# Reordering an attention and gated-convolution kernel with a list scheduler, whole-batch operations and full-array matmuls

## The chip, the cores and the metric

The kernel runs on one core of a Trainium2 chip. The metric is the device time of the whole program in microseconds (us), median of several executions, after its result was compared with the reference. For one core, an execution counts as slow when it is over 1.5% above the fastest of the same kernel. Engine names in profile lines: PE is TensorE (matmul), PEld its weight loads, DVE is VectorE, ACT is ScalarE, POOL is GpSimd (here it mostly issues loads), SP is SyncE. PSUM is the memory that the matmuls write to; these kernels use it in a few buffers, which ACT or DVE reads out before the next matmul may write there. The granted clock is the share of its full speed that the chip allowed TensorE. A matmul uses a part of TensorE's array of 128 rows and 128 columns; the size of that part is called its tile size.

## The reference

Eight batches, eight heads, 576 tokens, head size 64. Keys and values are averaged over groups of 8 tokens (72 remain), attention follows, and its output (512 columns a token) feeds a network with a three-tap convolution along the tokens as its gate.

```python
k_p = k.reshape(B, H, 72, 8, D).mean(axis=3)          # v_p likewise
attn = softmax(q @ k_p.T / sqrt(D))
x = (attn @ v_p)                                      # -> B, 576, 512
h = np.maximum(x @ w_in, 0)                           # 512 -> 1024 ("first layer")
gate = sigmoid(sum(conv_w[k] * shifted(h, k) for k in range(3)))
out = (h * gate) @ w_out                              # 1024 -> 512 ("second layer")
```

## The kernel before

Heads are handled in pairs. The order is written by hand: attention steps of batch b+1 stand between feed-forward steps of batch b. The parts that matter here, with cuts marked `# ...`:

```python
q_sb = qsb_pool.tile([96, S // 96, 2, D], BF16, name="q_sb")
for hh in range(2):
    nc.gpsimd.dma_start(out=q_sb[:, :, hh, :],
        in_=q[b, h0 + hh, :, :].rearrange("(c p) d -> p c d", p=96))   # runs of 256 bytes
# ... scores: each head of the pair uses 64 rows of the array
scps = sc_psum.tile([Sp, SC], FP32, name="scps", tag="sc")             # 2 buffers, SC = 288
nc.tensor.matmul(out=scps, lhsT=kT_sb[pb:pb + D, :], rhs=qT_sb[pb:pb + D, c0:c0 + SC], ...)
nc.scalar.activation(out=attnTs[hh][:, c0:c0 + SC], in_=scps, func=ACT.Exp, scale=...)
# ... attention times v; token tiles of 128,128,128,128,64
nc.vector.reciprocal(out=r_sb[0:usz], in_=avt[0:usz, sl, :, D])
for hh in range(2):
    nc.vector.tensor_scalar(out=x_pair[...], in0=avt[...], scalar1=r_sb[0:usz, hh:hh + 1], op0=OP.mult, ...)
# ... feed-forward: per block of 128 columns and per 288 tokens
#   first layer: 4 matmuls, relu on ACT;  convolution: 3 matmuls with diagonal weights, tanh on ACT
#   (the convolution's PSUM tiles share the two "sc" buffers with the scores)
for b in range(B):                     # the hand-written order, cut
    ffn_mm1(b, 2); ffn_conv(b, 1)
    attn_scores(nxt, 0)
    ffn_mm1(b, 3); ffn_conv(b, 2)
    attn_av(nxt, 0); attn_prep(nxt, 1); attn_loads(nxt, 3)
    # ...
```

The softmax here doesn't subtract the row's maximum and nothing guards it: scores larger than these inputs give would overflow.

## Time and profile before

Three executions: 328.02 to 329.11 us, median 328.87. From the page of the profiled execution (span; busy time and share of each engine; busy tenths of TensorE in 40 slices; the chain of work that ended last by engine and by line; groups of instructions with busy time, mean ns of one, and idle time in front of them; the issues of the q load):

```profile
span 327.8 us, 6104 instructions
PE 289.7 (88%) x2080; PEld 166.7 (51%) x2080; DVE 213.5 (65%) x904; ACT 188.3 (57%) x473; POOL 103.0 (31%) x196
...
PE   0054669999999999999999999999999999999995
...
PE 79%; DMA 11%; ACT 3%; DVE 3%; POOL 2%; issue 1%; ACTq 0%; POOLq 0%
PE hps L273 22%; PE cps L293 15%; PE scps L191 8%; DMA q_sb<-in_q_dram 5%; PE avps L223 5%; PE xt_ps L252 3%; PE q_ps L173 2%; DMA convw<-in_moe_conv_w_dram 2%; ACT xT L255 2%; DMA k_raw<-in_k_dram 2%; DMA w_in_sb_119<-in_moe_w_in_dram 1%; DVE osb L336 1%; DMA out_dram<-osb 1%; PE kT_ps L162 1%; DVE x_pair L234 1%
...
L234 DVE TENSOR_SCALAR x_pair<-avps,r_sb 128x64 bf16<-128x64 f32 (+1 forms) x320 | 72.3, 275 | 0.5
...
L198 ACT ACTIVATE attnT<-scps 72x288 bf16<-72x288 f32 x128 | 51.0, 405 | 12.8 <-PE scps L191 9.5
...
q_sb<-in_q_dram POOLq DMA_DIRECT2D x64, 72.0 KB, 3.8
```

Read it so. PE has 88% of the span and most of the chain: TensorE bounds the kernel. The slices show where it does not: about 50 us at the start. DVE spends its largest share on 320 normalizations of 64 columns, ACT runs exponentials in calls of 288 columns, and q comes in 64 small issues.

A busy share does not tell whether TensorE does useful work, because records of pipelined matmuls overlap and also cover waits inside the array. So I took the distance from one matmul's start to the next from the trace. Its usual value where nothing interferes is the floor of a kind of matmul. The sums include every wait in front of the next matmul.

```
kind                                    floor      before, us in all   after, us in all
first layer, convolution (288 columns)  122-125 ns      131.0              112.3
second layer (512 columns)              216 ns           74.4               63.8
scores (288 columns)                    122 ns           37.3               19.3
attention times v (65 columns)           33 ns           20.1               15.9
transposes of 128 columns                56 ns           (all three kinds of transposes: 53.2 before, 34.5 after)
```

In steady batches of the kernel before, a batch takes 35.8 us; its floors sum to about 28. The lines below are TensorE in one such stretch (timeline: start in us, duration, engine, line of the kernel, operation, output and inputs, rows*columns of the array used, count):

```profile
164.07 0.28 PE L273 MATMUL hps<-xT,w_in_sb_116 128*128 128x288 bf16 x1
164.37 0.28 PE L191 MATMUL scps<-qT_sb,kT_sb 64*72 64x288 bf16 x1
164.58 0.30 PE L273 MATMUL hps<-xT,w_in_sb_117 128*128 128x288 bf16 x1
164.71 0.29 PE L273 MATMUL hps<-xT,w_in_sb_118 128*128 128x288 bf16 x1
164.93 0.31 PE L191 MATMUL scps<-qT_sb,kT_sb 64*72 64x288 bf16 x1
165.17 0.30 PE L273 MATMUL hps<-xT,w_in_sb_119 128*128 128x288 bf16 x1
```

First-layer matmuls (128 rows) alternate with scores (64 rows). From 164.58 to 164.71, between two first-layer matmuls, the step is 0.13 us. The steps into and out of a scores matmul take 0.21 to 0.30.

### The profile page before, as it was taken

Reading aid. Unit: us, or ns where it says so; the run is one execution under the profiler, and the core shown is the slowest. Engines: PE = TensorE matmul, PEld = TensorE weight load, DVE = VectorE, ACT = ScalarE, POOL = GpSimd, SP = SyncE. Lnnn points to the kernel's source line nnn. Section 1 sums busy time; section 2 is a strip of 40 time slices with the busy share of each in tenths; the row PEclk is TensorE's granted clock in tenths of the full one; section 3 lists DMA queues with packets and bytes.
Section 4 is the critical chain, followed back from the end, with each engine's and each line's share of the span. In section 5 each row is a group of like instructions: output and inputs, shape, how many; then the busy total and the mean of one; then the engine's idle time right before and its main releaser. Section 6 shows DMA issues by size and latency. Waiting matters only on the chain.

```text
span 327.8 us, 6104 instructions
## 1 busy us (share of the span) xinstructions
PE 289.7 (88%) x2080; PEld 166.7 (51%) x2080; DVE 213.5 (65%) x904; ACT 188.3 (57%) x473; POOL 103.0 (31%) x196
## 2 busy tenths in 40 slices
PE   0054669999999999999999999999999999999995
PEld 0032335664566446654656456554566455645752
DVE  3523883677857785778757785777667866675452
ACT  1068425883398509872587429860787348852940
POOL 8068997752442226042513233110000000000000
PEclk9999999999999999999999999999999999999999
DMA  8999999995693659155964567133100120003003
GB/s 166 173 120 190 150 151 129 147 104 98 125 100 22 84 123 109 31 54 97 135 79 36 82 138 56 8 27 108 40 2 1 66 81 2 0 34 112 2 32 113
DMA packets 57342, 27.28 MB, mean 83 GB/s; under 512 B 42464, under 2 KB 51552, under 8 KB 57312
## 3 DMA queue, kind: packets, MB, share of 16 engines
q0 software_dynamic: 51968, 17.20, 48.2%
q10 hardware_dynamic: 2928, 5.38, 4.9%
q1 hardware_dynamic: 2416, 4.33, 4.5%
q8 instruction: 16, 0.26, 0.3%
q14 instruction: 14, 0.11, 0.1%
HBM read 32.52 MB, written 9.44 MB: 128 GB/s over the span
## 4 chain that ended last, share of the span: by engine, by line
PE 79%; DMA 11%; ACT 3%; DVE 3%; POOL 2%; issue 1%; ACTq 0%; POOLq 0%
PE hps L273 22%; PE cps L293 15%; PE scps L191 8%; DMA q_sb<-in_q_dram 5%; PE avps L223 5%; PE xt_ps L252 3%; PE q_ps L173 2%; DMA convw<-in_moe_conv_w_dram 2%; ACT xT L255 2%; DMA k_raw<-in_k_dram 2%; DMA w_in_sb_119<-in_moe_w_in_dram 1%; DVE osb L336 1%; DMA out_dram<-osb 1%; PE kT_ps L162 1%; DVE x_pair L234 1%
## 5 line engine op out<-in xcount | busy, mean ns | idle before, releaser
L234 DVE TENSOR_SCALAR x_pair<-avps,r_sb 128x64 bf16<-128x64 f32 (+1 forms) x320 | 72.3, 275 | 0.5
L293 PE MATMUL cps<-hT,dw 128*128 128x288 bf16 x384 | 60.3, 288 | 0.0
L255 ACT COPY xT<-xt_ps 128x576 bf16<-128x576 bf16 x32 | 20.4, 637 | 69.0 <-PE xt_ps L252 56.9
L121 POOL DMA_DIRECT2D q_sb<-in_q_dram x64 | 47.9, 759 | 35.7 <-PE q_ps L173 22.5
L231 DVE RECIPROCAL r_sb<-avps 128x2 f32<-128x2 f32 (+1 forms) x160 | 22.9, 161 | 54.4 <-PE avps L223 53.7
L198 ACT ACTIVATE attnT<-scps 72x288 bf16<-72x288 f32 x128 | 51.0, 405 | 12.8 <-PE scps L191 9.5
L280 ACT ACTIVATE hT<-hps 128x288 bf16<-128x288 f32 x128 | 52.0, 413 | 8.1 <-PE hps L273 3.7
L300 ACT ACTIVATE tg<-cps 128x288 bf16<-128x288 f32 x128 | 48.7, 412 | 7.4 <-PE cps L293 7.1
L191 PE MATMUL scps<-qT_sb,kT_sb 64*72 64x288 bf16 x128 | 39.1, 318 | 5.4 <-ACT attnT L198 4.8
L223 PE MATMUL avps<-v_aug,attnT 72*128 72x65 bf16 (+1 forms) x320 | 37.9, 202 | 5.3 <-DVE x_pair L234 4.2
L328 PEld LDWEIGHTS <-gT 128*128 128x128 bf16 (+1 forms) x320 | 27.8, 99 | 26.0 <-DVE gT L321 1.8
L293 PEld LDWEIGHTS <-dw 128*128 128x128 bf16 x384 | 35.3, 98 | 9.7 <-issue 0.2
L223 PEld LDWEIGHTS <-attnT 72*128 72x128 bf16 (+1 forms) x320 | 26.4, 102 | 26.0 <-issue 9.7
L273 PE MATMUL hps<-xT,w_in_sb_116 128*128 128x288 bf16 x128 | 37.5, 295 | 2.3 <-DVE osb L336 1.4
L273 PE MATMUL hps<-xT,w_in_sb_119 128*128 128x288 bf16 x128 | 36.4, 293 | 3.1 <-ACT xT L255 3.1
L273 PE MATMUL hps<-xT,w_in_sb_118 128*128 128x288 bf16 x128 | 37.5, 295 | 0.4 <-ACT xT L255 0.4
L273 PE MATMUL hps<-xT,w_in_sb_117 128*128 128x288 bf16 x128 | 37.4, 294 | 0.4 <-ACT xT L255 0.4
L178 ACT COPY qT_sb<-q_ps 128x576 bf16<-128x576 bf16 x32 | 20.5, 640 | 25.3 <-PE q_ps L173 25.1
L147 POOL MEMSET v_aug<- 72x2 bf16 x32 | 3.3, 110 | 100.2 <-PE avps L223 99.8
L191 PEld LDWEIGHTS <-kT_sb 64*72 64x72 bf16 x128 | 13.4, 109 | 29.2 <-issue 23.1
L252 PE MATMUL xt_ps<-ident_b,x_pair 128*128 128x128 bf16 (+1 forms) x160 | 26.5, 224 | 0.1
L113 POOL DMA_DIRECT2D v_raw<-in_v_dram x28 | 19.8, 707 | 11.5 <-DVE vt_3488 L149 2.6
(719 smaller groups left out, 429.3 us busy)
## 6 DMA issues: line engine op xcount, KB each, us to landing
q_sb<-in_q_dram POOLq DMA_DIRECT2D x64, 72.0 KB, 3.8
out_dram<-osb ACTq DMA_DIRECT2D x16, 256.0 KB
k_raw<-in_k_dram POOLq DMA_DIRECT2D x28, 144.0 KB, 4.5
v_raw<-in_v_dram POOLq DMA_DIRECT2D x28, 144.0 KB, 4.3
out_dram<-osb SPq DMA_DIRECT2D x8, 256.0 KB
out_dram<-osb POOLq DMA_DIRECT2D x8, 256.0 KB, 2.4
v_raw<-in_v_dram ACTq DMA_DIRECT2D x4, 288.0 KB
k_raw<-in_k_dram SPq DMA_DIRECT2D x4, 288.0 KB
```

The source lines that it names most:

```text
L121: nc.gpsimd.dma_start(out=q_sb[:, :, hh, :], in_=q[b, h0 + hh, :, :].rearrange("(c p) d -> p c d", p=96),)
L191: nc.tensor.matmul(out=scps, lhsT=kT_sb[pb:pb + D, :], rhs=qT_sb[pb:pb + D, c0:c0 + SC], start=True, stop=True,)
L198: nc.scalar.activation(out=attnTs[hh][:, c0:c0 + SC], in_=scps, func=ACT.Exp, scale=1.0 / (POOL * 8.0))
L223: nc.tensor.matmul(out=avt[0:usz, sl, hh, :], lhsT=attnTs[hh][:, u0:u0 + usz], rhs=v_aug[:, hh, :], start=True, stop=True,)
L234: nc.vector.tensor_scalar(out=x_pair[0:usz, hh * D:(hh + 1) * D], in0=avt[0:usz, sl, hh, 0:D], scalar1=r_sb[0:usz, hh:hh + 1], scalar2=Non ...
L252: nc.tensor.transpose(out=xt_ps[:, u0:u0 + usz], in_=x_pairs[i][0:usz], identity=ident_b[0:usz, 0:usz])
L255: nc.scalar.copy(out=xT, in_=xt_ps)
L273: nc.tensor.matmul(out=hps, lhsT=w_in_sb[dc][:, fb * P:(fb + 1) * P], rhs=xT_tiles[(b, dc)][:, c0:c0 + SC], start=(dc == 0), stop=(dc == n ...
L280: nc.scalar.activation(out=hT[:, fb, 1 + c0:1 + c0 + SC], in_=hps, func=ACT.Relu, scale=0.5)
L293: nc.tensor.matmul(out=cps, lhsT=dw[:, kk, i, :], rhs=hT[:, fb, c0 + kk:c0 + kk + SC], start=(kk == 0), stop=(kk == 2),)
L300: nc.scalar.activation(out=tg[:, c0:c0 + SC], in_=cps, func=ACT.Tanh, scale=0.5)
L328: nc.tensor.matmul(out=ops_[0:osz, :], lhsT=gT[:, fc, os0:os0 + osz], rhs=w_out_sb[fc], start=(fc == 0), stop=(fc == n_fb - 1),)
```

## The change

Intent: let a scheduler that runs at build time order all operations by engine, with estimated durations and a model of load arrival; make the operations larger (all heads of a batch or of a token tile at once, 576 columns a call on ACT); use only full-array matmuls, so that the array's tile size never changes; load each batch in three large loads with long runs. The core of a diff of 964 lines:

```diff
+class Planner:
+    N_PS = 4;  DMA_RATE = 220e3;  DMA_LAT = 2.2;  SEM = 0.12
+    def order(self):      # repeatedly: among operations whose inputs are planned, per engine the
+        # ...             # earliest start (0.02 us of slack), ties by priority; 4 PSUM buffers of 2 banks
-    nc.gpsimd.dma_start(out=q_sb[:, :, hh, :], in_=q[b, h0 + hh].rearrange("(c p) d -> p c d", p=96))
+    nc.gpsimd.dma_start(out=q_b[m], in_=flat_tokens(q, b))          # 9 KB in a row
-    lhsT=kT_sb[pb:pb + D, :],  rhs=qT_sb[pb:pb + D, c0:c0 + SC]      # 64 rows
+    lhsT=kTz[m][:, par, h*Sp:(h+1)*Sp],  rhs=qT[m][:, :, h*A:(h+1)*A]   # 128 rows, half of kTz is zero
-    for hh in range(2): nc.vector.tensor_scalar(out=x_pair[...], ...)
+    nc.vector.tensor_tensor(out=xx[i3] (128 x 512), in0=av_view(), in1=rr broadcast, op=OP.mult)
-    last token tile: 64 tokens (tokens 512 to 575)
+    last token tile: 128 tokens (448 to 575), overlapping the one before
-    relu / tanh / exp on 288 columns
+    relu / tanh / exp on 2 x 288 columns in one call
-    second layer: 5 token tiles a batch
+    second layer: 9 full token tiles for a pair of batches
+    # ... every operation: pl.add(name, engine(s), duration, fn, reads, writes, prio, ...)
+    with tc.manual_schedule():
+        for s, e, d, o in pl.order():
+            o.fn(e)
```

## The prediction

> **What bounds the kernel now.** TensorE. The page gives PE 289.7 us busy (88%), DVE 65%, ACT 57%, POOL 31%; PE has 79% of the chain that ended last. The timeline shows three stages: a prologue of 50 us, in which PE starts at 16 us, waits for q loads and small vector work, and runs first-layer matmuls at half pace (240 ns each, later 123); seven batches of 35.8 us; a last feed-forward of 24 us.
>
> Busy time hides the real limit, so I took start-to-start distances of matmuls from the trace. Undisturbed: 123 ns for 288 columns (first layer, convolution), 216 for 512 (second layer), 34 for attention times v, 56 for 128-column transposes. In the batch at 121.8 to 157.6 us these floors sum to 28.3 us. The other 7.5: 58 places where the array's tile size changes (64-row scores, 64-row or 64-column last token tiles, 64-column k transposes) lose 6.1 us over the floors, the other 200 lose 1.8. A first-layer matmul followed by a scores matmul takes 225 ns instead of 123, the way back 242. The Trainium skill, "TensorEngine Tiling (Array Packing)", Key Properties, says that a change of tiling mode drains TensorE; this trace agrees, about 0.1 us for each change.
>
> **What the change does.**
> - TensorE: scores contract over 128 zero-padded rows, the last token tile overlaps the one before, the output is tiled over batch pairs (36 tiles, not 40). Nearly all tile-size changes go. Count times floor: 512 and 384 at 123 = 63 + 47; 288 at 216 = 62; 128 scores at 123 = 16; 320 at 34 = 11; 160 and 144 transposes at 56 = 9 + 8; 48 at 42 = 2. Sum 218 us, 27.3 a batch (was 28.3 + 7.5).
> - ACT: 128x288 calls (405 to 413 ns) pair into 128x576 (estimate 0.65 us from the 0.64 us copy of that width): 192 x 0.65 = 125 us.
> - DVE: 320 normalizations at 275 ns become 40 of 128x512, estimate 0.69 each from the equal-sized output copy (28 us instead of 72); reciprocals 23 to 7 us; pooling sums 4.4 us a batch.
> - Copies that go to either add some 80 us. ACT and DVE end near 160 us each, under TensorE.
> - DMA: 256-byte q rows (64 issues) become 9 KB runs; POOL issues fall from 120 to 36; the software queue's 48% share should halve. In the steady state this is off the critical path; in the prologue it counts.
>
> **Prologue.** k, q, v and a quarter of the input weights are 4.1 MB; at the 171 GB/s of the first 16 us, or better with long rows, q and k land near 13 us; attention of batch 0 is paced by eight exponentials (5 us) and five normalization rounds (5 us). I expect the first feed-forward matmul near 28 us, saturated soon after (before: 50).
>
> **Sum.** 28 + (218 - 6 used before) + 1.5 of stall a batch (12) + 2 of half-rate start - 3 of overlap + 4 tail = 255 us. Range 244 to 270. Of the 74 us saved, about 20 come from the prologue, 43 from tile-size changes and other gaps, 8 from fewer columns.
>
> **Right if** the batch period is 28 to 30 us; scores matmuls follow each other and first-layer matmuls at about 123 ns; the chain is over 80% PE; ACT and DVE stay below 70%.
>
> **Wrong if** the strided q operand streams slower than 123 ns; the four two-bank PSUM buffers (estimate: 70% occupied) make PE wait because the fixed order assumes wrong durations; the loads of batch 0 land later; or merged ACT/DVE instructions cost more than estimated.
>
> Chances: faster 0.97, within 2% 0.02, slower 0.01.

## The result, and the profile after

After: 262.14 us median of four executions (260.94 to 262.55), before in the same rounds 328.44. The ratio is 0.796 (95% interval 0.793 to 0.800). Ratios in this document are the mean time of one kernel's fast runs over that of the other's in the same rounds, so not quite the ratio of the medians quoted. The page after, the same parts, and the granted clock by slice in tenths:

```profile
span 259.9 us, 4786 instructions
PE 235.1 (90%) x1985; PEld 166.9 (64%) x1985; DVE 126.8 (49%) x307; ACT 166.5 (64%) x271; POOL 25.6 (10%) x47
...
PE   0488997969999999999999999999999999999992
...
PEclk9995999968999999999999999999999999999999
...
PE 76%; ACT 13%; DVE 6%; DMA 3%; issue 1%; ACTq 0%; POOLq 0%
PE psf L478 24%; PE psf L531 23%; PE psf L497 18%; PE psf L402 5%; ACT tg L504 3%; DMA q_b<-in_q_dram 3%; ACT attnT L413 3%; DVE xx L443 2%; PE psb L385 2%; ACT osb L539 2%; PE psb L457 2%; PE psf L430 1%; ACT xT L463 1%; ACT qT L391 1%; ACT kTz L357 1%
...
L413 ACT ACTIVATE attnT<-psf 72x576 bf16<-72x576 f32 x64 | 39.7, 644 | 1.9 <-PE psf L402 1.9
...
L443 DVE TENSOR_TENSOR xx<-psf,rr 128x512 bf16<-128x512 f32 x40 | 26.8, 684 | 0.4
...
q_b<-in_q_dram POOLq DMA_DIRECT2D x7, 576.0 KB, 6.4
```

The first visible thing is the start: TensorE is saturated from the fifth slice (a slice is 6.5 us here), before from the seventh (of 8.2 us). Merged instructions cost less than the parts that they replace: an exponential of 576 columns 644 ns where two of 288 took 405 each, a normalization of 512 columns 684 ns where eight of 64 took 275 each. The second thing are dents in the seventh and ninth slice, between 39 and 58 us; in the ninth the clock shows a 6 (the 5 in the fourth slice belongs to the start). Nothing in the prediction speaks of them. Where a trace has no clock record, the page shows full clock. There is none before 16.4 us here, and none before 55.5 us in the kernel before, and until 16.2 and 55.1 us matmuls of 288 columns start 240 ns apart, half the later pace; so read no full clock from the first slices. The windows view of the changed kernel (stretch in us, its length, then busy time with count of PE, PEld, DVE, ACT, POOL, mean granted clock, DMA share, GB/s) shows it in figures:

```profile
core 0: us, PE busy (x) PEld busy (x) DVE busy (x) ACT busy (x) POOL busy (x), PEclk, DMA share, GB/s
0.00:23.30 23.30, 11.34 (x101) 8.60 (x102) 14.01 (x41) 12.45 (x23) 14.91 (x32) 0.93 1.14 197
23.30:38.80 15.50, 15.48 (x112) 11.58 (x112) 4.56 (x12) 9.67 (x15) 0.00 (x0) 0.89 1.19 206
38.80:62.10 23.30, 18.89 (x163) 12.74 (x161) 14.36 (x30) 12.66 (x21) 3.45 (x5) 0.85 0.91 159
62.10:90.00 27.90, 27.41 (x267) 21.81 (x265) 19.03 (x43) 23.81 (x41) 3.71 (x5) 1.00 0.67 107
90.00:120.00 30.00, 29.39 (x258) 20.81 (x256) 18.16 (x41) 21.45 (x36) 2.96 (x4) 1.00 0.78 141
```

From 23.3 to 38.8 us the feed-forward of batch 0 runs alone; from 38.8 to 62.1 the attention of batch 1, with only a few second-layer tiles beside it; only then do the two overlap as meant. PE is busy 18.9 of these 23.3 us, at a mean clock of 0.85.

The steady state looks as predicted. The same kind of stretch after the change (TensorE alone in the timeline):

```profile
121.29 1.14 PE L478 MATMUL psf<-xT,w_in 128*128 128x288 bf16 x8
122.27 0.41 PE L402 MATMUL psf<-qT,kTz 128*72 128x288 bf16 x2
122.51 0.91 PE L497 MATMUL psf<-hT,dw 128*128 128x288 bf16 x6
```

Eight first-layer matmuls take 0.98 us (121.29 to 122.27), two scores 0.24, and they follow each other without a gap.

Where the time went, worked out from start-to-start distances in both traces (time over the floors, us; floors for the same 2,080 and 1,985 matmuls; floors are rounded, so each column adds up to 0.3 us over its span):

```
                          before (span 327.8)    after (span 259.9)
sum of floors             223.5                  217.5
start to first steady
  feed-forward            43.1  (0 to 50.3)       17.6  (0 to 23.3)
all after that            57.5                    20.1, of which 9.0 from 38.8 to 62.1
after the last matmul      4.0                     5.0
```

So of the 67.9 us, 25.5 come from the start, 37.4 from the stretch after it, 6.0 from fewer matmul columns; 1.0 is lost at the end.

### The profile page after: what moved, and what is told of

Read it like the earlier page. It is cut to its first block, busy times and chain, and to the rows that moved or that the text cites. A ratio compares the mean times of both kernels' runs of the same rounds, so it can differ in the third digit from the quotient of the medians.

```text
span 259.9 us, 4786 instructions
## 1 busy us (share of the span) xinstructions
PE 235.1 (90%) x1985; PEld 166.9 (64%) x1985; DVE 126.8 (49%) x307; ACT 166.5 (64%) x271; POOL 25.6 (10%) x47
## 3 DMA queue, kind: packets, MB, share of 16 engines
q0 software_dynamic: 15024, 15.67, 38.5%
## 4 chain that ended last, share of the span: by engine, by line
PE 76%; ACT 13%; DVE 6%; DMA 3%; issue 1%; ACTq 0%; POOLq 0%
PE psf L478 24%; PE psf L531 23%; PE psf L497 18%; PE psf L402 5%; ACT tg L504 3%; DMA q_b<-in_q_dram 3%; ACT attnT L413 3%; DVE xx L443 2%; PE psb L385 2%; ACT osb L539 2%; PE psb L457 2%; PE psf L430 1%; ACT xT L463 1%; ACT qT L391 1%; ACT kTz L357 1%
## 5 line engine op out<-in xcount | busy, mean ns | idle before, releaser
L478 PE MATMUL psf<-xT,w_in 128*128 128x288 bf16 x512 | 74.4, 290 | 1.2 <-ACT xT L463 0.5
L531 PE MATMUL psf<-w_out,gT 128*128 128x512 bf16 x288 | 65.9, 379 | 1.4 <-DVE gT L514 1.1
L509 DVE TENSOR_SCALAR tg<-tg 128x576 bf16<-128x576 bf16 x64 | 20.1, 314 | 82.9 <-ACT tg L504 82.3
L478 PEld LDWEIGHTS <-w_in 128*128 128x128 bf16 x512 | 50.3, 99 | 15.7 <-issue 1.5
L497 PE MATMUL psf<-hT,dw 128*128 128x288 bf16 x384 | 57.9, 286 | 1.1 <-ACT kTz L357 1.0
L484 ACT ACTIVATE hT<-psf 128x576 bf16<-128x576 f32 x64 | 41.7, 652 | 18.0 <-PE psf L478 17.6
L531 PEld LDWEIGHTS <-gT 128*128 128x128 bf16 x288 | 27.9, 98 | 32.0 <-DVE gT L514 2.2
L504 ACT ACTIVATE tg<-psf 128x576 bf16<-128x576 f32 x64 | 41.5, 649 | 7.7 <-PE psf L497 2.4
L413 ACT ACTIVATE attnT<-psf 72x576 bf16<-72x576 f32 x64 | 39.7, 644 | 1.9 <-PE psf L402 1.9
L514 DVE TENSOR_TENSOR gT<-tg,hT 128x576 bf16<-128x576 bf16 x64 | 29.0, 453 | 1.5
L443 DVE TENSOR_TENSOR xx<-psf,rr 128x512 bf16<-128x512 f32 x40 | 26.8, 684 | 0.4
```

Source lines behind the costliest of these rows:

```text
L413: nc.scalar.activation(out=attnT[m][:, h, :].rearrange("p (c i x) -> p i c x", i=2, x=32), in_=slot(key)[0:Sp, :, 0:HC].rearrange("p i (c ...
L443: nc.vector.tensor_tensor(out=xx[i3].rearrange("p (g h e) -> p g h e", g=2, h=4), in0=av_view()[:, :, :, 0:D], in1=rr[i3].rearrange("p (g ...
L478: nc.tensor.matmul(out=t[:, i, 0:HC], lhsT=w_in[:, c, f * P:(f + 1) * P], rhs=xT[m][:, c, i * HC:(i + 1) * HC], start=(c == 0), stop=(c == ...
L484: nc.scalar.activation(out=hT[m][:, f, 2:S + 2].rearrange("p (i x) -> p i x", i=2), in_=slot(key)[:, :, 0:HC], func=ACT.Relu, scale=0.5)
L497: nc.tensor.matmul(out=t[:, i, 0:HC], lhsT=dw[:, f, kk, :], rhs=hT[m][:, f, 1 + kk + i * HC:1 + kk + (i + 1) * HC], start=(kk == 0), stop= ...
L504: nc.scalar.activation(out=tg[i3].rearrange("p (i x) -> p i x", i=2), in_=slot(key)[:, :, 0:HC], func=ACT.Tanh, scale=0.5)
```

## The experiments

Two theories about the steady part. A: changes of the array's tile size drained TensorE, and taking them away is what paid, whatever the order. B: the order of operations paid. Twelve kernels were run. All gave a correct result. Kernels of one call share the runs of the kernel before, whose median was 328.6 to 329.3 us in all calls.

```
kernel         median us   ratio to before, 95% interval   what it is
before         328.9       1
changed        262.1       0.796  0.793-0.800
b_pad          313.7       0.955  0.950-0.960   before + scores on 128 rows
b_full         301.4       0.918  0.914-0.922   before + no tile-size change at all
b_norm         296.4       0.903  0.900-0.906   b_full + merged normalization
a_rows64       266.8       0.812  0.808-0.816   changed, scores on 64 rows again
a_halves       262.8       0.800  0.797-0.803   changed, ACT calls of 288 columns again
a_q256         263.1       0.800  0.797-0.804   changed, q in 256-byte runs again
a_prio         313.9       0.952  0.947-0.957   changed, scheduler without a clock
a_hand         275.2       0.837  0.836-0.839   a_prio, two priorities moved by hand
a_early_rate   256.5       0.780  0.777-0.783   changed, batch 1 loaded and planned earlier
a_best2        245.2       0.746  0.743-0.748   a_early_rate + 2 of 8 convolution blocks on DVE
a_best3        244.9       0.745  0.744-0.747   3 blocks on DVE (1, 4, 7)
a_best4        242.1       0.736  0.733-0.739   3 blocks on DVE (1, 3, 5)
```

### b_pad: the kernel before, scores on 128 rows

```diff
+    kTz: three tiles [128, 2, 72], set to zero once, used in turn
-    tensor_copy(out=kT_sb[0:D, :], ...);  tensor_copy(out=kT_sb[D:2 * D, :], ...)
+    tensor_copy(out=kT_sb[0:D, 0, :], ...);  tensor_copy(out=kT_sb[D:2 * D, 1, :], ...)
-    lhsT=kT_sb[pb:pb + D, :],  rhs=qT_sb[pb:pb + D, c0:c0 + SC]
+    lhsT=kT_sb[:, hh, :],      rhs=qT_sb[:, c0:c0 + SC]
```

> The kernel before with one thing changed: scores contract over 128 zero-padded rows, so their matmuls no longer change the array's tile size. Theory A (tile-size changes cost TensorE about 0.11 us each and TensorE is the bound): 16 scores a batch with one change in and one out, 3.7 us a batch, about 26 us in seven batches: 303 us, range 298 to 310; the distance from a first-layer matmul to a scores matmul falls from 225 to 123 ns. Theory B (the gain of the change comes from order, merging and loads; the padding by itself gives nothing, as a matmul of 64 rows streams the same 288 columns): 325 to 330 us.

313.7 us: 15 us off, so theory B as stated falls, but A's 26 us is not there either. The step out of a scores matmul to the next first-layer matmul fell from 242 to 122 ns; the step into it, 230 ns in the mean, fell only to 199.

### b_full: no tile-size change left

```diff
-    s128: (0,128) (128,128) (256,128) (384,128) (512,64)
+    s128: (0,128) (128,128) (256,128) (384,128) (448,128)   # output of the last: its upper 64 rows
-    two transposes of ksum, 72 x 64 each
+    one transpose of ksum, 72 x 128
```

> As b_pad, and also full-size last token tiles (overlapping the one before) and one 128-column k transpose a head pair in place of two 64-column ones: no tile-size change is left in the steady state. Theory A: the whole 6.1 us a batch, some 43 us less than before: 286 us, range 280 to 294, leaving 24 us of the change's 66 us for all the rest. Theory B: 322 to 330 us.

301.4 us, between the two forecasts. The period of a batch fell from 35.8 to 31.8 us: 4.0, not 6.1. (The edit also saves one k transpose for each head pair and computes 64 tokens twice.) Where is the rest? The same stretch as shown of the kernel before, now in b_full (timeline; PE, and the ACT calls that matter):

```profile
86.93 0.78 ACT L303 ACTIVATE tg<-cps 128x288 bf16<-128x288 f32 x2
...
87.10 0.28 PE L276 MATMUL hps<-xT,w_in_sb 128*128 128x288 bf16 x1
...
87.39 0.28 PE L194 MATMUL scps<-qT_sb,kTz 128*72 128x288 bf16 x1
87.52 0.41 PE L276 MATMUL hps<-xT,w_in_sb 128*128 128x288 bf16 x2
87.71 1.18 ACT L201 ACTIVATE attnT<-scps 72x288 bf16<-72x288 f32 x3
...
87.76 0.28 PE L194 MATMUL scps<-qT_sb,kTz 128*72 128x288 bf16 x1
...
87.89 0.28 PE L276 MATMUL hps<-xT,w_in_sb 128*128 128x288 bf16 x1
...
88.17 0.28 PE L194 MATMUL scps<-qT_sb,kTz 128*72 128x288 bf16 x1
```

The first step, first-layer matmul to scores, is still 0.29 us (87.10 to 87.39), though no tile size changes; before it was 0.30. This score needs one of the two PSUM buffers that convolution and scores share, and ACT frees one when the first of the two tanh calls that start at 86.93 ends, at about 87.3. The steps out of scores, which were 0.21 to 0.25, are 0.12 to 0.13 (87.39 to 87.52, 87.76 to 87.89). But scores come 0.37 to 0.41 us apart, the pace of ACT's exponentials (three in 1.18 us). So part of what I had booked on tile-size changes was a wait for ACT and for a PSUM buffer at the same place, and removing the drain uncovered it. That the second wait is the cause of the missing 2 us a batch is read from this trace; no run gave those two pools more buffers.

### b_norm: one normalization a token tile

```diff
-    for hh in range(2): nc.vector.tensor_scalar(out=x_pair[..hh..], in0=avt[..hh..], scalar1=r_sb[:, hh:hh+1], ...)
+    nc.vector.tensor_tensor(out=x_pair as (2, D), in0=avt[:, sl, :, 0:D], in1=r_sb broadcast over D, op=OP.mult)
```

> As b_full, and the two normalizations of a token tile (275 ns each) become one over 128 columns (estimate 0.34 us from the 275 ns of 64 columns): DVE loses 160 x 0.2 = 33 us of 213. If DVE is off the critical path except in the prologue (30 to 50 us, where it was busy 80 to 86%): 296 us, range 292 to 300, with an unchanged period of 31.9 us a batch. If DVE's many small instructions hold up TensorE in the steady state too: 290 us or less, period 31 us or less.

296.4 us, as expected in total, but not for the expected reason alone. The first steady feed-forward matmuls came at 47.8 us instead of 50.7, and the period, expected to stay, fell to about 31.2 us. Of the 5.8 us between the two profiled executions (298.9 and 293.1 us), 2.5 are gained by the first layer of batch 1 and 3.3 after it: more than half is steady state, and hitting the total was in part luck.

### a_rows64: the changed kernel with scores on 64 rows

```diff
-    lhsT=kTz[m][:, par, ...],                        rhs=qT[m][:, :, ...]
+    lhsT=kTz[m][64 * par:64 * par + 64, par, ...],   rhs=qT[m][64 * par:64 * par + 64, :, ...]
```

> The changed kernel with scores back on 64 rows; same order, same number of instructions. Theory A: each pair of scores matmuls brings one change in and one out, 8 pairs a batch, 0.22 us a pair, seven batches: 12 us more, 274 us, range 268 to 280. Theory B: 262 us within 2.

4.6 us more, not 12. The timeline says why (TensorE; two scores between other matmuls):

```profile
62.51 1.16 PE L478 MATMUL psf<-xT,w_in 128*128 128x288 bf16 x8
63.59 0.31 PE L402 MATMUL psf<-qT,kTz 64*72 64x288 bf16 x2
63.84 0.92 PE L497 MATMUL psf<-hT,dw 128*128 128x288 bf16 x6
```

Going into the pair costs 0.1 us: from 62.51 to 63.59 is 1.08 us where eight first-layer matmuls otherwise take 0.98. But the pair and its way out take 0.25 us, as long as the two full-size matmuls did in the changed kernel (0.24). The starts of the two scores are 3 to 4 ns apart in 61 of 77 steps from one score to the next; in the changed kernel most are 121 to 123 ns apart. The two halves of the array work at the same time, which hands back the 0.12 us that the way out costs (243 ns from the second score to the next first-layer matmul, 122 without a change). In the steady batches the price is 0.8 us each (second-layer tiles of every second batch 59.0 to 59.7 us apart, 57.3 to 58.0 in the changed kernel). The Trainium skill, "TensorE: Matmul & The Clock Gate", Part 3, describes this overlap for matmuls in different row groups, with 4 ns between starts; the trace agrees, and I had not used it. In the kernel before, other work stood behind most scores; only 13 were followed directly by another, and only one of these steps was that short (3 ns). The others were 31 ns or more; twelve of the 13 lie in the start, so little of this overlap was at work in its steady batches.

### a_halves: ACT calls of 288 columns again

```diff
-    nc.scalar.activation(out=... 2 x 288 columns, in_=slot(key)[:, :, 0:HC], ...)
+    for i in range(2): nc.scalar.activation(out=... half i, in_=slot(key)[:, i, 0:HC], ...)   # relu, tanh, exp
```

> The changed kernel with exp, relu and tanh in two 288-column calls each, as before, in place of one of 576. ACT work rises by 192 times (2 x 0.41 - 0.65), 33 us, to about 200 us. If TensorE alone is the bound, the time stays at 262 to 268 us. If the merging on ACT is what paid, 280 us or more.

262.8 us: no difference. The test was weaker than planned: ACT's busy time rose from 166.5 to 175.6 us only, not by 33, since successive calls overlap in the records (426 ns each in the mean, but 128 of them in 46.5 us). It shows that merging the ACT calls is not where the gain came from in this order.

### a_q256: q in runs of 256 bytes again

```diff
-    nc.gpsimd.dma_start(out=q_b[m][:, j0:j1, :], in_=flat tokens j0 to j1)
+    for odd in range(2): nc.gpsimd.dma_start(out=q_b[m][:, odd tokens or even ones], in_=the same tokens)
```

> The changed kernel with each q load cut into even and odd tokens, so that its runs in memory are 256 bytes again, as before (same bytes, same layout in memory on chip, twice the issues for q). If loads are off the critical path in the steady state and count only in the prologue: q of batch 0 lands at 11 to 13 us rather than 8.5, the first feed-forward matmul comes 2 to 5 us later, total 263 to 270 us, period of a batch unchanged at 29. If the long runs pay all along: 275 us or more.

263.1 us, within the intervals no difference from the changed kernel, at the low edge of the expected range. The software queue's line (packets, MB, time of its packets as a share of 16 engines' span), first in the changed kernel, then here:

```profile
q0 software_dynamic: 15024, 15.67, 38.5%
```

```profile
q0 software_dynamic: 50768, 15.67, 56.7%
```

Three times the packets, 18 points more of the DMA engines' time, and next to nothing in the total: the last part of batch 0's q landed at 12.5 us instead of 10.1 and the first feed-forward matmul came at 24.7 instead of 23.3. In the kernel before, with the same 256-byte runs, the q loads of batch 0 landed only at 15.8 to 18.4 us; so run length is not what held them up there, and what did was not tried. The Trainium skill, "DMA: Bandwidth & Descriptors", Specifications, asks for transfers of 512 bytes or more for full rate; the packets' time here agrees, but full rate was not needed.

### a_prio: the scheduler without a clock

```diff
-    per engine: the earliest start within 0.02 us, then the lowest priority; the earliest of the engines
+    the lowest priority number among all operations whose inputs have been emitted
```

> The changed kernel, its scheduler without a clock: the next operation is the one of lowest priority number whose inputs have been emitted, wherever time stands (same operations, same priorities, same limit on PSUM buffers). If the timed order matters: transposes of attention outputs now stand directly behind the matmuls whose results they wait for, about 1 us of wait five times a batch, and scores of batch 1 stand before the feed-forward of batch 0 and wait for their loads: 290 us, range 275 to 310. If the gain comes from the form of the operations and any sane interleaving will do: 257 to 267 us.

313.9 us: above the expected range and worse than b_full, with every operation in its new form. The profiled execution was a slow one (its runs lie between 311.8 and 317.4), so I use its trace only to see what TensorE waits for. From its timeline and its waits (who waited for whom: us in all, times, longest):

```profile
120.04 0.42 PE L425 MATMUL psf<-vaug,attnT 72*128 72x65 bf16 x8
...
121.69 0.20 DVE L434 RECIPROCAL rr<-psf 128x8 f32<-128x8 f32 x1
121.93 0.69 DVE L438 TENSOR_TENSOR xx<-psf,rr 128x512 bf16<-128x512 f32 x1
122.67 0.29 PEld L452 LDWEIGHTS <-xx 128*128 128x128 bf16 x4 [2.33 <-DVE xx L438]
```

```profile
PE psb L452 <- DVE xx L438: 29.1, 23, 2.2
...
PE psb L346 <- DVE ksum L333: 15.8, 8, 4.8
```

At 120.04 the attention output of a token tile is computed, and right behind it in TensorE's queue stand the transposes of that same output, which need DVE's reciprocal and normalization first. No matmul further back went ahead of them, and TensorE stands idle for 2.21 us. Over the whole run it waits 29.1 us for such normalizations (23 times) and 15.8 us for DVE's sums in front of the k transposes (8 times).

The waits also cost clock. All four runs have a mean granted clock of 0.89 to 0.91, the changed kernel's 0.97 to 0.98. The clock line of a_prio's page:

```profile
PEclk9999999689959997599959998999958998799998
```

The profiled execution records 58 us at half clock within its span before the last matmuls, in eight stretches. The floors of the matmuls in them sum to 25.6 us, so half clock costs up to that much (an estimate; part of it is hidden by the waits). The 52 us between this kernel and the changed one are therefore waits and lost clock together, and no run parts the two.

### a_hand: two priorities moved

```diff
-    attn_k(b, o - 2.0);  k transpose and its copies: prio=pr;        output transposes: prio=pr + 0.3
+    attn_k(b, o - 3.0);  k transpose and its copies: prio=pr + 1.2;  output transposes: prio=pr + 1.05
```

> As a_prio (no clock), but with priorities of two operations moved by hand: the transposes of attention outputs come about two steps later than the matmuls that feed them, and the sums of k one step before their transposes. In a_prio TensorE stood 20.8 us between attention outputs and these transposes, and 14.7 us before k transposes. If these two adjacencies are what the timed order avoids: 278 us, range 270 to 288 (the wait for the loads of batch 1 stays). If it takes the clock everywhere: 295 us or more.

275.2 us. Still without a model of time, two priorities moved by hand take back 39 of the 52 us, and in the profiled execution the granted clock shows no fall before the last matmul. About half of what is left lies at the start: the first layer of batch 2 begins 6.6 us later than in the changed kernel, that of batch 7 13.5 us later. At the start there are 7.7 us of wait in front of the k transposes of batch 1, whose attention this order puts before the feed-forward of batch 0. So the scheduler's model of time is not magic: it keeps apart an operation and its consumer, and that was worth most of these 52 us.

### a_early_rate: the dent at 38.8 to 62.1 us

```diff
-    DMA_RATE = 220e3
+    DMA_RATE = 290e3
-    weights_in(-30);  loads(1, -20);  weights_out(-25)
+    weights_in(-30);  loads(1, -25);  weights_out(-20)
```

> The changed kernel with the loads of batch 1 issued ahead of the output weights, and the scheduler's assumed DMA rate 290 instead of 220 GB/s, so that it puts the attention of batch 1 into the feed-forward of batch 0. In the changed kernel that attention stood alone from 38.8 to 62.1 us, with 9.0 us of TensorE time over the floors. If the assumed arrival of loads is the cause: 254 us, range 251 to 258. If that stretch is bound by something else (the loads land no earlier and TensorE waits for them in the midst of the feed-forward): 259 us or more.

256.5 us, 5.6 less than the changed kernel. The windows view of the same two stretches as above, now in this kernel:

```profile
23.30:38.80 15.50, 14.79 (x118) 11.09 (x118) 6.51 (x14) 12.26 (x22) 2.15 (x3) 1.00 1.21 205
38.80:62.10 23.30, 22.75 (x224) 17.11 (x222) 16.05 (x37) 17.82 (x32) 2.94 (x4) 1.00 1.19 201
```

PE is busy 22.75 of the 23.3 us, at full clock: batch 1's attention now stands inside batch 0's feed-forward. In the first of the two stretches the matmuls still start 240 ns apart until 25.2 us; the trace has no clock record there, so its 1.00 is not to be trusted. In the changed kernel the scheduler, which books loads one after another at 220 GB/s behind 2.1 MB of output weights, thought that the keys of batch 1 came later than they did; they landed 18.3 us after their issue at 10.4, at 28.7, and DVE first touched them at 39.65. The two edits were not run apart. But the scheduler itself can be run without the chip. In the changed kernel it books the keys of batch 1 for 43.4 us, with the new rate alone for 33.6, with the new load order alone for 33.8, with both for 26.3, and only with both does it put scores of batch 1 before the last first-layer block of batch 0, in the order that the trace shows. What one edit alone would give on the chip is not shown.

### a_best2, a_best3, a_best4: a faster version

With TensorE the bound and DVE at 49%, some convolution blocks can move. Each of them is then computed on DVE instead of six matmuls:

```diff
+    if f in FS:      # (2, 6), then (1, 4, 7), then (1, 3, 5)
+        for kk in range(3): tensor_scalar(out=ct[kk], in0=hT[..shifted kk..], scalar1=cw[..], op0=OP.mult)
+        # ... two tensor_tensor additions into ct[0], tanh on ACT from ct[0]
+    last pair of batches: mm2(p, (7,)) and mm2(p, (8,)) stored apart
```

> As a_early_rate, and 2 of the 8 convolution blocks go from TensorE (six matmuls of 123 ns) to DVE (three scalings at 0.31 us and two additions at 0.46, as DVE instructions of this size took), and the last output pair is stored in two parts. If TensorE is the only bound, 2 x 0.735 x 8 = 12 us less TensorE time, about 1 us less tail: 241 us, range 237 to 247, DVE near 156 us. If the order or DVE binds by then: 248 us or more.

> As a_best2, with three instead of two convolution blocks of eight on DVE: TensorE 5.9 us less, DVE 13 us more (to about 161 us). If TensorE is still the only bound: 239.5 us, range 238 to 242. If DVE's part of each block now sets the pace: 244 us or more.

> As a_best3, but the three DVE convolution blocks are 1, 3 and 5 instead of 1, 4 and 7. In a_best3 block 7, the last of a batch, was one of them, and TensorE waited 2.5 us for it in front of the last output tiles. If that wait is what ate the gain over a_best2: 242 us, range 240.5 to 243.5. If DVE delays blocks wherever they stand: 244.5 us or more.

245.2, 244.9 and 242.1 us; a_best3 missed its range. The third block on DVE gave nothing while block 7, the last of a batch, was among them: TensorE lost 2.5 us in front of the last output tiles waiting for it. With blocks 1, 3 and 5 the time fell to 242.1, about half of the 5.9 us that a third block was to save. The busy shares of that kernel:

```profile
span 240.2 us, 4613 instructions
PE 216.5 (90%) x1841; PEld 151.5 (63%) x1841; DVE 157.8 (66%) x421; ACT 167.9 (70%) x278; POOL 25.7 (11%) x47
```

It beats both kernels, at 0.736 of the time before.

## Why the prediction was right or wrong

The prediction was 255 us with a range of 244 to 270; 262.1 was measured. The direction and the bound were right, two terms of the sum were off and partly cancel. In the prediction's own sum: start 23.3 instead of 28 us, floors after it 212 as predicted, stalls 20.1 instead of 11, tail 5.0 instead of 4, together 260; and the device time is 2 us over the profiled span (261.9 and 259.9), which the sum left out. That it came within 7 us is in part luck, since the short start pays half of the missed stalls.

- **TensorE bounds the kernel, and stays the bound: right.** ACT has 64% and DVE 49% of the span (below 70%, as said; DVE's 126.8 us are well under the 160 foreseen). The chain is 76% PE; the prediction's test of over 80% was missed. The floors sum to 217.5 us; predicted 218.
- **The period: right.** Second-layer tiles of every second batch come 57.3 to 58.0 us apart, 29 us a batch; predicted 28 to 30. Scores and first-layer matmuls follow each other at 122 ns; the strided q operand costs nothing extra.
- **The start: right in kind, too long.** Predicted 28 us, measured 23.3. k had landed at 8.0 us and the last third of q at 10.1; the estimate of 13 used the 171 GB/s of the kernel before, and here the first 23.3 us show 197 GB/s. a_q256 shows that the long runs, which the prediction counted on here, matter little (1.4 us). What else shortened the start (all heads of a token tile at once instead of four passes of small dependent steps, at half pace, from 30 to 50 us) is read from the traces; only merged normalizations (b_norm, about 3 us of it) were tried alone.
- **The step that failed: "1.5 of stall a batch (12) + 2 of half-rate start - 3 of overlap", 11 us. It measured 20.1.** From 62 us on it holds: 9.3 us over the floors in 193 us. But 9.0 us more lie in one place that I did not foresee, 38.8 to 62.1 us, where the fixed order left batch 1's attention alone. The prediction named the danger ("the fixed order assumes wrong durations") but looked for it in the PSUM buffers; the wrong assumption was a load's arrival (keys of batch 1 booked for 43.4 us, landed at 28.7). Half clock from 54.0 to 60.8 us, which followed the waits, is part of the 9.0 us: up to 2.8, the floors of the matmuls in that stretch (an estimate). The order of instructions could be read before the run, and it shows only first-layer and convolution matmuls in the feed-forward of batch 0, no scores between them.
- **"43 from tile-size changes and other gaps": the sum is close (37.4), the split was wrong.** Tile-size changes alone are worth 27 us in the kernel before (b_full), not 6.1 a batch over seven batches, because at many of these places ACT and a PSUM buffer were late too; and put back alone into the changed kernel they cost 4.6 us. The order is worth more: without it the same operations take 313.9 us, lost clock included. The parts do not add up to the whole, since each wait hides others.
- **Loads off the critical path in the steady state: right.** a_q256: the share of the software queue rises by 18 points and the period stays at 57.3 to 58.0 us for two batches. That this share would halve was wrong: 48.2% before, 38.5% after.
- **Merged ACT calls: the cost estimate was right (0.65 us predicted, 0.644 to 0.652 measured), their gain none** (a_halves).

What stays open: how much each of the many smaller merges gave at the start, what held up the q loads in the kernel before, how the loss in a_prio parts into waits and clock, and what load order and assumed rate would each give alone in a_early_rate.

## What to carry to other kernels

Before booking the time at a costly place on one cause, look what else ends there: two waits at the same place are worth only one of them when one is taken away. In an engine's queue, keep a few independent operations between a producer and its consumer; here two priorities moved by hand did most of what the scheduler's model of time did. Short waits can cost twice, when the granted clock falls after them: look at it before putting a loss on the waits alone. A scheduler is as good as its model of the loads: check the first batches, where its guesses about arrival decide what may overlap.

## What the Trainium skill lacked or had wrong

- "TensorEngine Tiling (Array Packing)", Key Properties, says that changing the tiling mode drains TensorE but gives no size. In these runs: 94 ns on the way into a pair of 64-row matmuls and 120 ns on the way out (216 and 242 ns between starts instead of 122), and when two matmuls in both row halves follow each other, 3 to 4 ns apart, their overlap pays the way out back (a_rows64, 4.6 us in all instead of 12).
- "TensorE: Matmul & The Clock Gate", Part 1, has in its table of two states that the clock falls to half after an idle window of about 3.4 us. The intervals agree (3.41, 6.83, 27.31 us in the changed kernel), and so does the size (only 1.0 and 0.5). But the window need not be idle: in the changed kernel the clock fell after one in which PE was busy 1.95 of 3.41 us, with waits of at most 0.36 us. The page's own later section on a second failure mode tells of falls after frequent short idle times, but not how much idle time it takes. The windows view (columns as above) shows that window and the next:

```profile
50.57:53.98 3.41, 1.95 (x24) 1.14 (x24) 0.16 (x2) 2.96 (x6) 0.00 (x0) 1.00 1.05 141
53.98:57.40 3.42, 2.52 (x34) 2.19 (x31) 2.99 (x9) 0.92 (x2) 0.00 (x0) 0.50 1.12 228
```

- No page says when such a partly busy window is too idle, and the busy time of the records does not decide it. In a_prio, windows with 1.20 to 1.60 us of 3.41 busy were followed by half clock, but one with 1.54 and one with 1.78 were not, though both are emptier than the one above.
